# Attention and a two-layer product on one core: the first tiles of all batches first, wider late score runs, turned q left permuted

## The chip, the core and the metric

The kernel runs on one core of one Trainium2 chip. Its engines are TensorE (PE, matmuls), VectorE (DVE), ScalarE (ACT), GpSimd (POOL) and SyncE (SP); POOL, SP and ACT can also issue DMA transfers. The metric is the time of the program on the device in microseconds (us), as the median of several runs. The span of a profile goes from the first to the last instruction; the rest of the time lies around it.

## The reference

The inputs are q, k and v of 4 batches, 8 heads, 768 positions and 64 values a head. Attention is masked: a query sees the first 8 positions and the 96 positions up to its own, with a bias that falls with distance. The result goes through two matrix products with `h - tanh(h)` between them.

```python
scores = scale * np.matmul(q, k.transpose(0, 1, 3, 2))
dist = np.where(is_global & ~is_local, float(n_local), np.abs(rel))
scores = np.where(is_global | is_local, scores - slopes * dist, -1e9)
a = softmax(scores)
x = (a @ v).transpose(0, 2, 1, 3).reshape(3072, 512)
h = x @ w_in            # 512 x 2048
return (h - np.tanh(h)) @ w_out   # 2048 x 512
```

## The kernel before, in words

**Units.** The 3072 rows are 24 units of 128 positions, six a batch, taken in order: u = 0 to 23, with u % 6 the place i in the batch. A unit with i = 0 needs one block of keys (its own), every other unit two: its own (o = 0) and that of the unit before it (o = 1). The 8 global keys and values are copied from the batch's first unit over the first 8 places of the block (`a_K`, L436, `a_V`, L439, both through the copy helper at L302).

**Steps of a unit.** q and k are loaded by POOL's DMA queue with a cast to bf16 (`load_rows` L365 for units under `ROWS` = 4, which puts four consecutive positions in one partition's row; `load_natural` L368 for the others; unit 0 alone comes as f32 through SP and ACT and is cast by an engine). They are turned, so that the head's values lie along the partitions: units 0 to 5 by PE (`a_T`, L388, L392, L382) with a copy out of PSUM (`a_Te`, lines L300 on ACT and L302 on DVE), units 6 to 23 by a DMA transpose that SP issues (`a_DT`, L403). For units under `ROWS` the turned data come out in an order in which the four positions of a row are apart, and `a_Te` puts them in order while it copies. Then scores (`a_S`, L422; two heads at a time in the two halves of the partitions), exponential (`a_E`, L429), product with a mask that holds exp(bias) (`a_M`, L433; units under `BIASED` = 3 have the bias added on PE by `bias`, L346, instead), the product with v (`a_AV`, L448, with a column of ones that gives the sum), reciprocal and product (`a_R`, L456 and L457), and x turned again (`a_X`, L468, with a copy for units under 8; a DMA transpose, `a_DX`, L479, from unit 8 on). The three masks are made from PSUM at the start (`bm` through L346, `em` at L351).

**The two products.** Units form groups: 0 and 1 alone, then pairs. `m1` (L490) gives h for a group in pieces of 512 columns of one PSUM bank (128-column matmuls for a single unit, 256 for a pair), ACT takes tanh (L500), DVE subtracts (L506), `m2` (L515) sums 16 matmuls of 512 columns for a unit in one bank, ACT or DVE copies the bank out (L300, L302), and POOL or, for the last three units, SP stores it (L524). w_in comes in five pieces (in0 to in4: 2, 2, 4, 4 and 4 of the 16 row blocks), w_out in four (out0 to out3).

**The order.** It is made ahead by a planner (`Plan`, L17 to L191) that plays the operations through with a duration for each, a priority (`pri`, lower first), what they take and give back (the eight PSUM banks, in pairs for scores and AV; buffers; DMA lanes, eight for POOL's loads and stores, eight for SP's), and two rings for POOL's and SP's transfers that share the DMA engines equally. A transfer counts as landed after its issue, a lag, its work (`W_...`, L557), a tail and a slack (L21 and L22; it fades in from 20 to 30 us and out from 180 to 190 us). What the planner gives is the order of each engine's queue; on the chip each engine takes its queue strictly in that order and waits on semaphores. The list `first` (L576) sets POOL's loads by hand; then come kq and v of units 6 on. `AHEAD` (L558) lets the scores of unit u start only when `m1` has been issued up to unit u - 4.0, `T_AHEAD` (L562) lets its turn start from u - 6.0 on. `HOLD` keeps single operations back till a time, and dummy matmuls (L732) keep PE busy at the start. Numbers of buffers: `NK` 5 for loaded q and k, `NQK` 8 for turned ones, `NV` 10 for v, five for the exponentials, three for x.

Of the kernel before, what the change touches and what calls it, by code (L numbers as in the profile page):

```python
# [16 lines left out]
class Plan:  # L17
# [3 lines left out]
    SLACK_DMA = 2.5  # L21
    SLACK_DT = 6.0  # L22
# [33 lines left out]
    def run(self, free):  # L56
# [71 lines left out]
        while events:  # L128
            now, _, what, key = heapq.heappop(events)
            if what == "done":  # L130
                for g in ops[key]["give"]:
                    left[g] -= 1
                    if left[g] == 0:
                        h, part = g
                        p, ids = holds[h]
                        for i in ids if part is None else [ids[j] for j in part]:
                            avail[p].append((now, i))
                drop("done", key)
            elif what == "issued":
                drop("issue", key)  # L140
            elif what == "enter":
                flow(now)
                rings.setdefault(ops[key]["ring"], []).append([key, ops[key]["work"]])
                again(now)
            elif what == "flow":
                if key != version:
                    continue
                flow(now)
                for r in rings.values():
                    while r and r[0][1] <= 1e-9:  # L150
                        k, _ = r.pop(0)
                        push(now + ops[k]["tail"] + margin(now, self.SLACK_DT if k[0] in ("T", "Xe") else self.SLACK_DMA), "done", k)
                again(now)
            if events and events[0][0] <= now + 1e-9:
                continue
            for e in (PE, ACT, DVE, POOL, SP):
                if busy[e] > now + 1e-9:
                    continue
                best = None
                for k in ready[e]:  # L160
                    o = ops[k]
                    if best is not None and (o["pri"], o["n"]) >= best[0] or self.hold.get(k, 0.0) > now + 1e-9:
                        continue
                    if fits(o, now):
                        best = ((o["pri"], o["n"]), k)
                if best is None:
                    continue
                k = best[1]
                o = ops[k]
                for x in o["eng"]:  # L170
                    ready[x].remove(k)
                for h, p, n in o["take"]:
                    ids = self.choose(p, n, avail[p], now)
                    avail[p] = [g for g in avail[p] if g[1] not in ids]
                    holds[h] = (p, ids)
                us = o["us"] if e is o["eng"][0] or o["us2"] is None else o["us2"]
                if e is PE and now < self.cold:
                    us *= 2.0
                end = now + us
                busy[e] = end  # L180
                start[k] = now
                order.append((now, k, e))
                push(end, "free", e)
                push(end, "issued", k)
                if o["ring"] is None:
                    push(end + self.LAT[e] + margin(end, self.SLACK_ENG), "done", k)
                else:
                    push(end + o["lag"], "enter", k)
# [6 lines left out]
def kernel(  # L195
# [30 lines left out]
    PG = P // R4  # L226

    ROWS = 4
# [3 lines left out]
    BIASED = 3  # L232
    SINGLE = 2
    NK, NV, NQK = 5, 10, 8
# [109 lines left out]
    def bias(holder, o, m, stop):  # L344
        for a in range(2):
            nc.tensor.matmul(  # L346
                bank(holder, 2 * o + a), dist[:, m, :], slopes[:, a * NP : (a + 1) * NP, :], start=True, stop=stop
            )
# [10 lines left out]
    def rows_of(src, u):  # L359
        b, i = u // NQ, u % NQ  # L360
        return src[b, :, i * P : (i + 1) * P, :]
# [14 lines left out]
    def a_T(u):  # L376
        s = buf(("kq", u))
        for j in (1, 0):
            if u >= ROWS:
                t = bank(("tr", u, j)).bitcast(BF16)  # L380
                for p in range(NP):
                    nc.tensor.transpose(t[:, p * P : (p + 1) * P], s[:, j, p * P : (p + 1) * P], ident)  # L382
                continue
            t = bank(("tr", u, j))
            for r in range(R4):
                o = t[:, r * P : (r + 1) * P]
                if u < HW:
                    nc.tensor.matmul(o, s[:, j, r * P : (r + 1) * P], turn, start=True, stop=True)  # L388
                    continue
                for hh in range(2):  # L390
                    c = (hh * R4 + r) * Dh
                    nc.tensor.matmul(o[hh * Dh : (hh + 1) * Dh], s[:, j, c : c + Dh], turn, start=True, stop=True)  # L392

    def a_Te(e, u, j):
        t = bank(("tr", u, j))
        d = buf(("qk", u))[:, j]
        if u >= ROWS:
            copy(e, d, t.bitcast(BF16)[:, 0 : NP * P].rearrange("q (p f) -> q p f", p=NP))
        else:
            copy(e, d.rearrange("q p (g r) -> q r p g", r=R4), t.rearrange("q (r p g) -> q r p g", r=R4, p=NP))  # L400
# [6 lines left out]
    def blocks(u):  # L407
        return (0, 1) if u % NQ else (0,)

    def mask_of(u, o):  # L410
        return 2 if o else min(u % NQ, 1)

    def a_B(u):
        for o in blocks(u):
            bias(("s", u), o, mask_of(u, o), False)

    def a_S(u):
        for o in blocks(u):
            for p in range(NP):
                for hh in range(2):  # L420
                    r = slice(hh * Dh, (hh + 1) * Dh)
                    nc.tensor.matmul(  # L422
                        bank(("s", u), 2 * o + hh)[:, p * P : (p + 1) * P], buf(("qk", u - o))[r, 1, p, :],
                        buf(("qk", u))[r, 0, p, :], start=u >= BIASED, stop=u >= BIASED or p == NP - 1,
                    )

    def a_E(u, o):
        d = buf(("p", u, o)).rearrange("k (a h) f -> k a (h f)", a=2)
        nc.scalar.activation(d, banks(("s", u), 2 * o, 2 * o + 1), AF.Exp, bias=0.0, scale=scale)  # L429
# [5 lines left out]
    def a_K(e, u):  # L435
        copy(e, buf(("qk", u))[:, 1, :, 0:G], buf(("qk", u - u % NQ))[:, 1, :, 0:G])  # L436

    def a_V(e, u):
        copy(e, buf(("v", u))[0:G, :, 0:Dh], buf(("v", u - u % NQ))[0:G, :, 0:Dh])  # L439
# [4 lines left out]
    def a_AV(u):  # L444
        t = av(u)
        for h in range(H):
            for o in blocks(u):
                nc.tensor.matmul(  # L448
                    t[:, h // (H // 2), h % (H // 2), :], buf(("p", u, o))[:, slot(h), :], buf(("v", u - o))[:, h, :],
# [73 lines left out]
    def store(e, u, c0, c1):  # L523
        eng(e).dma_start(out=out[u * P : (u + 1) * P, c0:c1], in_=buf(("ot", u))[:, c0:c1])  # L524
# [9 lines left out]
    W_HW, W_ROW, W_NAT, W_WT, W_ST, W_DT, W_DX = 0.75, 0.69, 1.0, 2.54, 0.68, 1.2, 0.6  # L534
    AHEAD = 4.0
    BM_PRI = (45, -90, -89)
    EM_PRI = (45, 15, 25)
    HOLD = {('bm', 0): 20.0, ('M', 3, 0): 21.3}
    T_AHEAD = 6.0
# [11 lines left out]
    for m in range(3):  # L551
        op(("bm", m), PE, 0.44, lambda e, m=m: bias(("mk", m), 0, m, True),
# [23 lines left out]
    first = "v0 kq1 v1 kq2 v2 v3 in0 kq3 in1 in2 kq4 out0 v4 kq5 out1 in3 in4 v5 out2 out3"  # L576
# [36 lines left out]
    FLEX = (ACT, DVE)  # L613
    for u in range(NU):
        i = u % NQ
        b0 = u - i
# [5 lines left out]
        sdep = [("issue", go[-1])] if go else []  # L622
        kq_give = [(("kq", u), None)]
        if u < PE_T:
            op(("T", u), PE, 0.46, lambda e, u=u: a_T(u), after=tdep + [("turn" if u < ROWS else "ident",)],
               take=[(("tr", u, 0), "bank", 1), (("tr", u, 1), "bank", 1), (("qk", u), "qk", 1)], give=kq_give, pri=base)
            op(("Te", u, 1), (ACT, DVE), 0.6, lambda e, u=u: a_Te(e, u, 1), us2=0.72 if u < ROWS else 0.43, after=[("T", u)],
               give=[(("tr", u, 1), None)], pri=base)
            op(("Te", u, 0), (DVE, ACT), 0.7 if u < ROWS else 0.43, lambda e, u=u: a_Te(e, u, 0), us2=0.6,
               after=[("T", u)], give=[(("tr", u, 0), None)], pri=base)  # L630
            have = [("Te", u, 0), ("Te", u, 1)]
        else:
            op(("T", u), SP, 1.25, lambda e, u=u: a_DT(u), after=tdep,
               take=[(("qk", u), "qk", 1), (("lane", "T", u), "hlane", 1)], give=kq_give + [(("lane", "T", u), None)],
               pri=base, ring=SP, work=W_DT, lag=0.0, tail=D_TAIL)
            have = [("T", u)]
        nb = len(blocks(u))
        if u < BIASED:
            op(("B", u), PE, 0.43 * nb, lambda e, u=u: a_B(u), after=[("first",), ("slopes",), ("issue", ("S", u - 1)) if u else None, ("issue", ("T", u)) if u else None],
               take=[(("s", u), "bank", 2 * nb)], pri=base)  # L640
        last_user = i == NQ - 1
        s_give = [(("qk", u - 1), None)] if i >= 2 else []
        if last_user:
            s_give += [(("qk", u), None)]
        op(("S", u), PE, 0.23 * nb + 0.18, lambda e, u=u: a_S(u),
           after=have + sdep + [("K", u - 1) if i >= 2 else None, ("B", u) if u < BIASED else None],
           take=[] if u < BIASED else [(("s", u), "bank", 2 * nb)], give=s_give, pri=base)
        for o in blocks(u):
            op(("E", u, o), ACT, 1.03, lambda e, u=u, o=o: a_E(u, o), after=[("S", u)],
               take=[(("p", u, o), "pr", 1)], give=[(("s", u), (2 * o, 2 * o + 1))], pri=base)  # L650
# [3 lines left out]
        if 1 <= i < NQ - 1:  # L654
            op(("K", u), DVE, 0.16, lambda e, u=u: a_K(e, u), after=[("S", u)],
# [5 lines left out]
        if i >= 2:  # L661
            a_give += [(("v", u - 1), None)]
        if last_user:
            a_give += [(("v", u), None)]
        op(("AV", u), PE, 0.24 * nb, lambda e, u=u: a_AV(u),
           after=pm + [("lv", u), ("V", u - 1) if i >= 2 else None],
# [11 lines left out]
        else:  # L678
            op(("Xe", u), SP, 1.2, lambda e, u=u: a_DX(u), after=[("R", u)] + x_dep,
               take=x_take + [(("lane", "X", u), "hlane", 1)], give=[(("x", u), None), (("lane", "X", u), None)],  # L680
               pri=base, ring=SP, work=W_DX, lag=0.0, tail=D_TAIL)
# [106 lines left out]
```

## Time and profile before

| what | value |
|---|---|
| time, median of 3 runs | 215.45 us (215.19 to 215.81) |
| time of the profiled execution | 215.66 us |
| its span | 213.7 us |
| PE, DVE, ACT, POOL busy | 204.3, 128.0, 120.0, 79.9 us |
| first row of L490 / of L515 on PE | 16.69 / 25.14 us |
| last PE matmul ends | 210.86 us |
| transposes on SP: of q and k / of x | 18 / 16 |
| matmuls of L346 (bias) recorded | 14 of 16 |

The page of the profile lists the busy time of each engine, 40 equal slices of the span with a digit for the busy tenths, the chain of work that ended last, and the costliest groups of instructions: source line, engine, operation, tiles, count, busy time and mean duration, then the idle time of the engine just before them with what ended it. L12 is line 12 of the kernel. A matmul's own duration holds the time through the array, so durations of neighbours overlap; what one costs in a stream is read from the chain, where pieces follow each other without overlap. A few matmul records are missing from the trace. PEld is the load of weights into the array, which runs beside the matmuls.

### The profile page before, as it was taken

The page shows a single profiled execution, that of the slowest core. Times are in us where ns is not written, and L with a number is a line of the kernel's source. Part 1 is how long each engine was busy: PE and PEld are TensorE (multiplying, and loading weights), DVE is VectorE, ACT ScalarE, POOL GpSimd, SP SyncE. Part 2 cuts the span into 40 slices and gives each one's busy share as a digit, 9 for nine tenths or more (in the row PEclk, how much of TensorE's full clock was granted, in tenths as well). Part 3 has the DMA queues.
Part 4 walks back from the last instruction along what each step waited for, and adds up shares of the span by engine and source line. Part 5 has one row for each costly group of instructions (what it writes and reads, how often), then busy time and mean ns, then how long its engine had stood idle before and what let it go on. Part 6 is the DMA issues. An engine that isn't in the chain of part 4 may idle for free.

```text
span 213.7 us, 5020 instructions
## 1 busy us (share of the span) xinstructions
PE 204.3 (96%) x2043; PEld 141.3 (66%) x2062; DVE 128.0 (60%) x256; ACT 120.0 (56%) x177; POOL 79.9 (37%) x105
## 2 busy tenths in 40 slices
PE   7679899999999999999999999999999999999994
PEld 2448686858656966856856865856856866848643
DVE  6588974834666985974881880853881880813600
ACT  4869855556576674753923923753923923715421
POOL 8996364467476454624537252001002002011000
PEclk9999999999999999999999999999999999999999
DMA  5999999999999999999999999915513012102012
GB/s 115 157 182 188 183 207 198 168 145 155 186 148 196 139 174 127 160 138 143 179 113 207 120 186 191 205 29 130 94 25 93 35 25 81 44 0 98 3 49 98
DMA packets 103478, 27.32 MB, mean 128 GB/s; under 512 B 94944, under 2 KB 101856, under 8 KB 103456
## 3 DMA queue, kind: packets, MB, share of 16 engines
q0 software_dynamic: 74624, 18.88, 90.6%
q1 hardware_dynamic: 28560, 7.87, 28.9%
q8 instruction: 16, 0.26, 0.5%
q10 hardware_dynamic: 272, 0.26, 0.5%
q14 instruction: 6, 0.05, 0.1%
HBM read 27.26 MB, written 6.29 MB: 157 GB/s over the span
## 4 chain that ended last, share of the span: by engine, by line
PE 86%; POOL 6%; DMA 5%; issue 1%; ACT 0%; POOLq 0%
PE ps L515 39%; PE ps L490 38%; DMA w_out_bf<-in_moe_w_out_dram 5%; PE ps L422 5%; PE ps L448 4%; POOL kq L365 2%; POOL vb L368 2%; POOL w_in_bf L371 1%; POOL kq L368 1%; PE ps L468 0%; PE ps L382 0%; POOL rel L306 0%; ACT ot L300 0%; POOLq L306 0%; POOLq L769 0%
## 5 line engine op out<-in xcount | busy, mean ns | idle before, releaser
L490 PE MATMUL ps<-xT,w_in_bf 128*128 128x256 bf16 (+1 forms) x832 | 89.5, 264 | 0.1
L515 PE MATMUL ps<-w_out_bf,g 128*128 128x512 bf16 (+2 forms) x383 | 86.1, 370 | 1.3 <-DMA w_out_bf<-in_moe_w_out_dram 0.3
L490 PEld LDWEIGHTS <-w_in_bf 128*128 128x128 bf16 x832 | 75.1, 98 | 12.0
L506 DVE TENSOR_TENSOR g<-ps,th 128x512 bf16<-128x512 f32 x96 | 64.0, 685 | 31.2 <-ACT th L500 30.1
L500 ACT ACTIVATE th<-ps 128x512 f32<-128x512 f32 x96 | 55.9, 605 | 23.8 <-PE ps L490 23.1
L515 PEld LDWEIGHTS <-g 128*128 128x128 bf16 x400 | 36.9, 98 | 38.8 <-issue 0.4
L429 ACT ACTIVATE pr<-ps 128x1024 bf16<-128x1024 f32 x44 | 42.9, 1023 | 8.1 <-PE ps L422 8.0
L300 ACT COPY ot<-ps 128x512 f32<-128x512 f32 (+2 forms) x22 | 12.5, 567 | 54.2 <-PE ps L515 54.2
L524 POOL DMA_DIRECT2D out_dram<-ot x21 | 11.8, 561 | 68.6 <-ACT ot L300 61.9
L433 DVE TENSOR_TENSOR pr<-pr,mk 128x1024 bf16<-128x1024 bf16 x39 | 26.4, 687 | 8.9 <-ACT pr L429 8.8
L368 POOL DMA_DIRECT2D vb<-in_v_dram x24 | 21.7, 905 | 12.1 <-DMA kq<-in_q_dram 2.6
L368 POOL DMA_DIRECT2D kq<-in_k_dram x20 | 17.7, 885 | 16.8 <-DMA kq<-in_k_dram 8.5
L368 POOL DMA_DIRECT2D kq<-in_q_dram x20 | 17.6, 882 | 11.7 <-DMA kq<-in_k_dram 5.3
L457 DVE TENSOR_TENSOR x<-ps,rden 128x512 bf16<-128x512 f32 x24 | 16.6, 692 | 0.8
L448 PEld LDWEIGHTS <-pr 128*128 128x128 bf16 x352 | 13.6, 97 | 3.7 <-ACT pr L429 1.1
L448 PE MATMUL ps<-vb,pr 128*128 128x65 bf16 x352 | 14.6, 193 | 0.8 <-DVE qk L302 0.8
L422 PEld LDWEIGHTS <-qk 64*128 64x128 bf16 x352 | 10.2, 94 | 7.2 <-issue 5.4
L456 DVE RECIPROCAL rden<-ps 128x8 f32<-128x8 f32 x24 | 5.0, 207 | 12.2 <-PE ps L448 11.5
L302 DVE COPY qk<-qk 128x32 bf16<-128x32 bf16 x16 | 2.8, 176 | 15.5 <-PE ps L422 15.3
L422 PE MATMUL ps<-qk 64*128 64x128 bf16 x192 | 9.5, 218 | 2.3 <-ACT qk L300 1.8
L302 DVE CAST qk<-ps 128x512 bf16<-128x512 f32 x5 | 6.3, 1305 | 2.9 <-PE ps L388 1.6
L422 PE MATMUL ps<-qk,qk 64*128 64x128 bf16 x160 | 7.8, 216 | 0.0
(43 smaller groups left out, 59.0 us busy)
## 6 DMA issues: line engine op xcount, KB each, us to landing
out_dram<-ot POOLq DMA_DIRECT2D x21, 256.0 KB, 7.2
vb<-in_v_dram POOLq DMA_DIRECT2D x24, 128.0 KB, 11.2
kq<-in_k_dram POOLq DMA_DIRECT2D x23, 128.0 KB, 11.3
kq<-in_q_dram POOLq DMA_DIRECT2D x23, 128.0 KB, 10.5
w_out_bf<-in_moe_w_out_dram POOLq DMA_DIRECT2D x4, 512.0 KB, 12.3
w_in_bf<-in_moe_w_in_dram POOLq DMA_DIRECT2D x3, 512.0 KB, 12.1
w_in_bf<-in_moe_w_in_dram POOLq DMA_DIRECT2D x2, 256.0 KB, 6.4
out_dram<-ot SPq DMA_DIRECT2D x2, 256.0 KB, 2.0
```

What stands on the lines that cost most here:

```text
L300: nc.scalar.copy(out=out, in_=in_)
L368: eng(e).dma_start(out=dst, in_=rows_of(src, u).rearrange("h p d -> p h d"))
L422: nc.tensor.matmul(bank(("s", u), 2 * o + hh)[:, p * P : (p + 1) * P], buf(("qk", u - o))[r, 1, p, :], buf(("qk", u))[r, 0, p, :], start=u ...
L429: nc.scalar.activation(d, banks(("s", u), 2 * o, 2 * o + 1), AF.Exp, bias=0.0, scale=scale)
L433: nc.vector.tensor_tensor(out=t, in0=t, in1=mk[:, mask_of(u, o)], op=ALU.mult)
L448: nc.tensor.matmul(t[:, h // (H // 2), h % (H // 2), :], buf(("p", u, o))[:, slot(h), :], buf(("v", u - o))[:, h, :], start=o == 0, stop=o ...
L457: nc.vector.tensor_tensor(out=buf(("x", u)).rearrange("q (a h) d -> q a h d", a=2), in0=t[:, :, :, 0:Dh], in1=rden.to_broadcast([P, 2, H / ...
L490: nc.tensor.matmul(t[:, (f - f0) * n : (f - f0 + 1) * n], w_in_bf[j][:, c, fo : fo + P], x[:, c, 0:n], start=(c == 0), stop=(c == CD - 1),)
L500: nc.scalar.activation(h_view(buf(("th", g, f0)), g, m), h_view(bank(("h", g, f0)), g, m), AF.Tanh, bias=0.0, scale=1.0)
L506: nc.vector.tensor_tensor(out=buf(("g", g))[:, f0 : f0 + m, 0:n], in0=h_view(bank(("h", g, f0)), g, m), in1=h_view(buf(("th", g, f0)), g, ...
L515: nc.tensor.matmul(bank(part)[:, 0 : c1 - c0], buf(("g", g))[:, f, t * P : (t + 1) * P], w_out_bf[f // FJ][:, f % FJ, c0:c1], start=(f == ...
L524: eng(e).dma_start(out=out[u * P : (u + 1) * P, c0:c1], in_=buf(("ot", u))[:, c0:c1])
```

## The change

Six things are changed.

1. The units are taken in another order: `turn_of` lists the first tiles of the four batches first (u = 0 to 3), then the other five of each batch. `nth` is the place in the batch, `back` the unit before in the batch, `head` the batch's first unit. So the first four units have one block each, and the first tiles' k and v are kept until their batch is through (`NQK` 11, `NV` 12). `BIASED` is 4; the mask for first tiles is not made, since no unit from 4 on uses it.
2. From unit 16 on, scores run in threes of blocks: of three units, two runs instead of three. Scores of a block have banks of their own (`("s", u, o)`).
3. `ROWS` is 5. For these units k is turned straight into its order (PE writes PSUM with a step of four), q stays in the turned order, `a_Te` copies both without rearranging, and `a_S` reads q through `queries`, which jumps 128 elements between neighbouring columns.
4. POOL's loads come in another order at the start.
5. The planner's figures are new: slacks 1.5 and 3.0 instead of 2.5 and 6.0, with 2.5 more for a transpose when another ring is at work; transposes have 0.8 of lag and works of 1.66 and 1.18 instead of 1.2 and 0.6; a store 0.6 instead of 0.68; a turn on PE 0.69 instead of 0.46; `AHEAD` 4.5, `T_AHEAD` 5.5; other priorities for the masks, other `HOLD`s.
6. The planner may keep an operation that needs many banks ahead of lower ones (`KEEP` = 9); no operation takes more than six.

```diff
-    SLACK_DMA = 2.5
-    SLACK_DT = 6.0
+    SLACK_DMA = 1.5
+    SLACK_DT = 3.0
+    SHARED = 2.5
+    KEEP = 9
...
-                        push(now + ops[k]["tail"] + margin(now, self.SLACK_DT if k[0] in ("T", "Xe") else self.SLACK_DMA), "done", k)
+                        more = margin(now, self.SLACK_DMA)
+                        if k[0] in ("T", "Xe"):
+                            shared = any(x for y, x in rings.items() if y is not e)
+                            more = margin(now, self.SLACK_DT) + (self.SHARED if shared else 0.0)
+                        push(now + ops[k]["tail"] + more, "done", k)
...
-    ROWS = 4
+    ROWS = 5
-    BIASED = 3
+    BIASED = 4
-    NK, NV, NQK = 5, 10, 8
+    NK, NV, NQK = 5, 12, 11
+    turn_of = sorted(range(NU), key=lambda t: (t % NQ > 0, t))
+    nth = [t % NQ for t in turn_of]
+    back = [turn_of.index(t - 1) if t % NQ else None for t in turn_of]
+    head = [turn_of.index(t - t % NQ) for t in turn_of]
+    THREES = 16
...
+        if u < THREES or u + 2 >= NU:
+            runs.append([(u, o) for o in blocks_of(u)])
+            u += 1
+        else:
+            runs += [[(u, 0), (u, 1), (u + 1, 0)], [(u + 1, 1), (u + 2, 0), (u + 2, 1)]]
+            u += 3
...
-                o = t[:, r * P : (r + 1) * P]
+                o = t.rearrange("q (p g r) -> q r p g", r=R4, p=NP)[:, r] if j else t[:, r * P : (r + 1) * P]
...
-            copy(e, d.rearrange("q p (g r) -> q r p g", r=R4), t.rearrange("q (r p g) -> q r p g", r=R4, p=NP))
+        copy(e, d, t if u < ROWS else t.bitcast(BF16)[:, 0 : NP * P])
+
+    def queries(u, p, r):
+        d = buf(("qk", u))[r, 0]
+        if u < ROWS:
+            return d.rearrange("q p f -> q (p f)").rearrange("q (r p g) -> q p g r", r=R4, p=NP)[:, p]
+        return d[:, p]
...
-                        buf(("qk", u))[r, 0, p, :], start=u >= BIASED, stop=u >= BIASED or p == NP - 1,
+                        queries(u, p, r), start=u >= BIASED, stop=u >= BIASED or p == NP - 1,
...
-    W_HW, W_ROW, W_NAT, W_WT, W_ST, W_DT, W_DX = 0.75, 0.69, 1.0, 2.54, 0.68, 1.2, 0.6
-    AHEAD = 4.0
-    BM_PRI = (45, -90, -89)
-    EM_PRI = (45, 15, 25)
-    HOLD = {('bm', 0): 20.0, ('M', 3, 0): 21.3}
-    T_AHEAD = 6.0
+    W_HW, W_ROW, W_NAT, W_WT, W_ST, W_DT, W_DX = 0.75, 0.69, 1.0, 2.54, 0.6, 1.66, 1.18
+    AHEAD = 4.5
+    BM_PRI = (-88,-90,-89)
+    EM_PRI = (45,2,35)
+    HOLD = {('m2', 1, 0, 2): 43.5, ('g', 2, 6): 31.8, ('Te', 1, 0): 8.0, ('Te', 1, 1): 8.0}
+    T_AHEAD = 5.5
...
-    for m in range(3):
+    for m in range(3) if BIASED < 4 else (1, 2):
...
-    first = "v0 kq1 v1 kq2 v2 v3 in0 kq3 in1 in2 kq4 out0 v4 kq5 out1 in3 in4 v5 out2 out3"
+    first = "kq1 v0 v1 kq2 kq3 v2 v3 kq4 in0 in1 out0 in2 in3 v4 out1 kq5 in4 v5 out2 out3"
...
+                op(("S", n), PE, 0.23 * len(xs) + 0.18, lambda e, xs=xs: a_S(xs), after=s_after[n] + s_dep[first_u],
+                   take=s_take[n], give=s_give[n], pri=10.0 * first_u)
...
-               pri=base, ring=SP, work=W_DT, lag=0.0, tail=D_TAIL)
+               pri=base, ring=SP, work=W_DT, lag=0.8, tail=D_TAIL)
-               pri=base, ring=SP, work=W_DX, lag=0.0, tail=D_TAIL)
+               pri=base, ring=SP, work=W_DX, lag=0.8, tail=D_TAIL)
```

## The prediction

> **What bounds the kernel now.** I read the busy times and the 40 slices first, then the table of stretches, then TensorE's rows in order of time, then the DMA issues.
>
> ```profile
> PE 204.3 (96%) x2043; PEld 141.3 (66%) x2062; DVE 128.0 (60%) x256; ACT 120.0 (56%) x177; POOL 79.9 (37%) x105
> ...
> PE   7679899999999999999999999999999999999994
> ```
>
> TensorE (PE) is busy 96% of the span; the rest lies in the first five slices and in the last. The table of stretches (its first columns are the stretch, its length, and PE's busy time) says the same in microseconds:
>
> ```profile
> 5.00:16.70 11.70, 8.34 (x140) 5.52 (x139) 7.59 (x13) 9.12 (x11) 11.17 (x16) 1.00 1.59 169
> 16.70:25.10 8.40, 7.52 (x148) 6.86 (x147) 7.35 (x17) 7.94 (x12) 4.00 (x6) 1.00 1.80 181
> 25.10:45.00 19.90, 19.70 (x220) 15.09 (x223) 13.24 (x25) 11.03 (x18) 11.13 (x13) 1.00 1.67 188
> 45.00:140.00 95.00, 94.33 (x947) 65.83 (x956) 62.50 (x118) 56.43 (x85) 45.13 (x57) 1.00 1.82 162
> 140.00:210.90 70.90, 70.58 (x587) 46.84 (x589) 33.98 (x60) 33.13 (x54) 4.32 (x8) 1.00 0.20 55
> ```
>
> From 25.1 to 210.9 PE lacks 0.2 + 0.7 + 0.3 = 1.2 us in 185.8. So the end is fixed by when PE becomes full and by how much work is then left. Nothing can be won after 25.1 except by removing PE work; much can be lost there. TensorE's rows of the first stretch (start, time, what, in brackets the idle time before and who ended it):
>
> ```profile
> 7.86 0.40 PE L422 MATMUL ps<-qk 64*128 64x128 bf16 x8 [1.48 <-ACT qk L300]
> ...
> 14.12 0.64 PE L448 MATMUL ps<-vb,pr 128*128 128x65 bf16 x16 [0.78 <-DVE qk L302]
> ...
> 16.69 1.09 PE L490 MATMUL ps<-xT,w_in_bf 128*128 128x128 bf16 x16
> ...
> 20.90 0.38 PE L346 MATMUL ps<-slopes,dist 128*128 128x512 bf16 x1
> ...
> 25.14 1.89 PE L515 MATMUL ps<-w_out_bf,g 128*128 128x512 bf16 x7 [0.33 <-DMA w_out_bf<-in_moe_w_out_dram]
> ```
>
> Two things are seen. Up to 16.7 PE waits for turned q and k. From 16.7 to 25.1 it has the first matrix product of units 0 and 1 only; the second starts when the first piece of w_out lands. For prices I take pieces of the chain that ended last, where PE runs without a gap:
>
> ```profile
> 41.11 0.48 PE ps L448 x16
> ...
> 45.29 3.45 PE ps L515 x16
> 48.74 6.99 PE ps L490 x64
> ...
> 132.34 0.33 PE ps L422 x8
> ...
> 139.15 0.55 PE ps L422 x16
> ```
>
> A 512-column matmul takes 0.216 us, a 256-column one 0.109, a 128-column one of L490 half of that (0.055). A score run of one block costs 0.33, of two 0.55, so 0.11 fixed and 0.22 a block. AV (L448) costs 0.48 for two blocks, and 0.26 for one (the chain has 0.26 for x8). A transposition of x costs 0.22 (x4).
>
> **The stretch 16.7 to 25.1 of before.** Counted work: 64 small matmuls of L490, 3.50; two score runs, 1.10; two AV, 0.96; two x, 0.44; the transposes of unit 4, 0.45; the two bias matmuls for mask 0, 0.43. Sum 6.88 of 8.40, so 1.52 are lost to waits and unfilled starts.
>
> **First tiles first.** Units 0 to 3 are now the first tiles of the four batches, with one block each: four blocks stand before group 2 is complete, where before it was seven. Bias matmuls fall from 16 (10 for units 0 to 2, 6 for masks) to 12 (8 and 4). The mask-0 pair at 20.9 goes, which is 0.43 in a stretch that is nearly full; the other two go from waiting time and count nothing. ScalarE loses one mask exponential (1.02), VectorE gains one mask product (0.69); neither is near its limit (56% and 60%).
>
> **When the data come.** Each load, asked singly for issue and landing: v0 is issued at 1.36 and lands at 7.0, then k1 7.9, q1 8.5, v1 9.6, k2 10.2, q2 10.8, v2 11.8, v3 12.7, in0 14.4, k3 15.1, q3 15.8, in1 17.1, in2 19.6, k4 20.4, q4 21.3, out0 25.1. Up to v3 the lag is 5.0 to 5.6, so POOL's issues (0.70 for rows, 0.88 natural, 0.45 more for the first) set the pace; later the transfer does: 0.7 a row load, 1.3 for 256 KB, 2.5 for 512 KB (out0: 3.8). In the new order I get k1 6.6, q1 7.6, v0 8.7, v1 9.5, k2 10.0, q2 10.7, k3 11.4, q3 12.2, v2 13.1, v3 14.0, k4 14.7, q4 15.4, in0 16.9, in1 18.2, out0 20.7 to 22.0, in2 23.2 to 24.5. So w_out comes 3 to 4 us earlier, w_in 1.1 later, and 2.5 more us of loads for units 3 and 4 stand ahead of it.
>
> PE can be full from about 17.8 (before, L490 started 0.4 ahead of in1 as well). Is unit 3 ready? q3 12.2, turn 0.64, latency 0.2, copy 0.69, scores 0.33, exponential 1.03 and 0.2, AV 0.26 and 0.2, reciprocal and product 0.90, x 0.42, copy 0.6: about 17.7; groups 0 and 1 have 1.75 us of L490 before it, so there is some slack. Done by 17.8 and not by 16.7 in before: unit 4's turn (0.45), scores 4 x 0.33 + 0.55 = 1.87 against 1.43, AV 1.04 against 0.74, two more x (0.44): 1.63 us of work for 1.1 us of time, +0.53.
>
> From 17.8 the supply is: L490 on in0 and in1 for four units, 16 x 4 x 4 x 0.055 = 3.5, with AV and x of unit 4 (0.7), to 22.0; out0 is there, 16 x 0.216 = 3.45, to 25.4; in2 is there, 3.5. In3 (about 26), out1 (29), in4 (34), out2 (37), out3 (40) each bring another 3.5, so arrival stays ahead. Of the 1.52 lost I let 0.6 come back: the joint at 22 is tight, and four open w_out sums hold four of eight PSUM banks. Bounds are 0 and 1.52.
>
> **Turned q stays permuted.** The casts go from a strided write to a contiguous one:
>
> ```profile
> L302 DVE CAST qk<-ps 128x512 bf16<-128x512 f32 x5 | 6.3, 1305 | 2.9 <-PE ps L388 1.6 <-PE ps L392 1.3
> L300 ACT CAST qk<-ps 128x512 bf16<-128x512 f32 x3 | 3.9, 1299 | 0.0
> ...
> L302 DVE COPY ot<-ps 128x512 f32<-128x512 f32 x3 | 2.1, 692 | 0.5 <-PE ps L515 0.5
> ```
>
> So about 0.6 off each of eight casts; unit 4's two go from 0.42 and 0.59 to about 0.65 each. This shortens the chain of a unit, but data arrive too late for it to move 17.8, so I count nothing. If loads came sooner it would be worth 0.6. The price moves to PE: k is written into PSUM with steps of four elements (36 half or whole matmuls), and q is read with a jump of 128 elements at each column (48 score matmuls). No row of before has a strided PE operand. The nearest rows are the casts above, where a step of four costs a factor 1.9; the other end is no cost, and a gain is excluded, because the same columns pass. At 1.9, scores 48 x 0.034 x 0.9 = 1.5 and turns 36 x 0.04 x 0.9 = 1.3. Nearly all of it falls before 17.8, where PE has some 3.4 us idle, so I take 0, and keep up to 1.5 for the range.
>
> The Trainium skill, page "Advanced Engine Details and Errata", section "Memory Cachelines", speaks against this part: SBUF is fast only where accesses share a 16-byte line, and any PSUM pattern that is not contiguous slows matmuls significantly. It gives no figure, and the casts' 1.9 is the only size that this trace offers for a stride; the rule is rival 1 below.
>
> **Late runs of three.** From unit 16 on, two sets of three units need two runs of three blocks instead of three of two: 2 x (0.77) against 3 x 0.55, 0.11 a set, 0.22 in all, on the path. Such a run wants three free bank pairs of four. Its exponentials free them at 1.03 steps, so one bank is left to L490 for about 1.25 us, which is at most 0.4 lost a run, 1.6 for four runs; at these places w_out work, which needs one bank, can stand beside, so I take 0.
>
> **Transposes planned anew.** This changes only the order: a score run may follow its transpose by one unit of MLP progress instead of two (4.5 against 5.5, before 4.0 against 6.0; a unit is some 7.9 us). The planned time to landing becomes 1.25 + 0.8 + 1.66 + 0.95 + 3.0 = 7.7 alone, and 11.8 when loads share the engines. Measured from issue to landing:
>
> ```profile
> qk<-kq SPq DMA_TRANSPOSE x16, 10.1
> xT<-x SPq DMA_TRANSPOSE x11, 8.4
> ```
>
> This is the answer for 40 to 138 us, with 11.5 as the longest; after 138 it is 3.8 and 2.4. The planned 11.8 covers it, so I count 0 while loads run.
>
> **Sum.** 1.52 - 0.6 + 0.43 + 0.53 + 0.22 = 2.1 us. The profiled execution took 215.66 with a span of 213.7; the span should become 211.6. The median, 215.45, is 0.2 below that execution; I take the gain off the median: **213.4**.
>
> **Rivals.** (1) Strides cost PE time that is not hidden: the factor 1.9 lengthens unit 3's chain by 0.3 for the turn, 0.3 for scores, and unit 4's turn and scores by 0.8, which fall near 17.8. Gain 2.1 - 1.1 = 1.0: 214.4. For it: the casts; against it: idle PE until 17.8. This is what the rule cited above makes of the time. (2) Weights come late: w_in 19.0 and out0 with its 3.8 again, so that the whole 1.52 is lost again, only elsewhere; 2.1 - 0.9 - 0.8 = 0.4: 215.0. For it: POOL is busy 11.17 of 11.7 us from 5 to 16.7, so any delay there moves all loads. (3) Slower: the score run stands in PE's order before its transpose has landed. In before it starts 13 to 18 us after the issue; one unit less is 5 to 10, and only the plan's wait holds it back. Where the plan takes the engines to be free and they are not, PE stalls 10.1 - 7.7 = 2.4, and behind it wait all of PE's matmuls. One such wait eats the gain; two give 215.45 - 2.1 + 4.8 = 218.1. Against it: loads fill the DMA engines until 138 us on the chip, and in a plan with nearly the same work too. (4) That the change does less than said: the start is bound by loads alone, and PE's lost time stays; this ends as (2).
>
> **Numbers.** Forecast 0.60 (212.2 to 214.7); rival 1 0.12; rivals 2 and 4 0.13; rival 3 0.15. A measurement of this kernel tells 0.3%, 0.65 us, from no change. Faster: 0.60 + 0.12 = 0.72; within: 0.13; slower: 0.15. The range goes from 212.2 (nothing comes back of the 1.52, and unit 4's AV done early) to 215.9, which leaves out rival 3 and little more.
>
> **What would show it.** Right: PE's first row of L490 near 17.8, of L515 before 22.5, full from there; casts near 0.65; L422 rows of three blocks taking 0.77; no PE idle time over 0.3 us after 25. Wrong: L422 rows of units 0 to 4 with more than 0.045 us a matmul (rival 1); idle PE ended by w_in or w_out after 18 (rival 2); idle PE ended by a transpose's qk or xT between 45 and 138 (rival 3).

## The result, and the profile after

The changed kernel takes 216.56 us (median of 22 runs), the kernel before in the same runs 215.83: ratio 1.0037, 95% interval 1.0024 to 1.005. It is slower by 0.7 us where 2.1 faster was forecast, and lies above the stated range (212.2 to 215.9). The first profiled execution (span 213.6, time 215.74) is the lowest of the 22, so by itself it hides the loss; a second one lies higher and is shown in experiment 5.

The table of stretches, whose rows answer to those of before (PE's busy time is the number behind the stretch's length, the granted clock the third from the right):

```profile
5.00:16.70 11.70, 10.89 (x129) 6.11 (x128) 4.91 (x9) 7.81 (x12) 11.70 (x17) 1.00 1.54 150
16.70:25.10 8.40, 8.15 (x103) 6.23 (x102) 6.27 (x13) 6.11 (x9) 3.88 (x5) 1.00 1.26 201
25.10:45.00 19.90, 19.80 (x239) 15.33 (x239) 13.09 (x24) 10.06 (x16) 10.01 (x13) 1.00 1.78 183
45.00:140.00 95.00, 94.31 (x977) 66.56 (x986) 63.47 (x121) 58.28 (x85) 45.74 (x57) 1.00 1.93 161
140.00:210.90 70.90, 70.38 (x599) 47.24 (x603) 37.25 (x67) 33.00 (x51) 4.35 (x8) 1.00 0.19 57
```

PE is now busy 10.89 of 11.7 us before 16.7, against 8.34, and 8.15 of 8.4 in the next stretch, against 7.52; from 25.1 on it is as full as before. The time did not go into waits. PE's rows in order of time show what it was busy with (L449 is the score line, L517 the first product, L542 the second; other kernels have other line numbers):

```profile
7.31 1.03 PE L449 MATMUL ps<-qk 64*128 64x128 bf16 x8
...
8.81 1.04 PE L449 MATMUL ps<-qk 64*128 64x128 bf16 x8
...
18.47 1.04 PE L449 MATMUL ps<-qk 64*128 64x128 bf16 x8 [0.20 <-DVE qk L326]
19.32 1.06 PE L449 MATMUL ps<-qk,qk 64*128 64x128 bf16 x8
20.31 1.07 PE L517 MATMUL ps<-xT,w_in_bf 128*128 128x128 bf16 x16
...
24.08 1.89 PE L542 MATMUL ps<-w_out_bf,g 128*128 128x512 bf16 x7
```

The same in pieces of the chain that ended last, which from 3.1 on is mostly PE: a run of one block for unit 0, of two for unit 4, of two for unit 5 (whose q is not permuted), and of three.

```profile
7.38 0.96 PE ps L449 x8
...
18.47 1.91 PE ps L449 x16
...
37.64 0.55 PE ps L449 x16
...
124.81 0.78 PE ps L449 x24
```

Sixteen score matmuls take 1.91 us where q is read with jumps and 0.55 where it is not. Over the 48 of units 0 to 4, the steps from one matmul to the next, without waits, add up to 5.71 us, against 2.01 in the first experiment below: 0.119 each against 0.042. Each run has some 0.1 more at its end in both; in the longer runs of the later stream a step is 0.034. The first product starts at 20.31, not at 17.8, although its second piece of w_in had landed at 19.1.

The casts are what they were to be: 0.69 us on VectorE and 0.59 on ScalarE, where the kernel before has 1.31 and 1.30. So part 3 moved a cost from two engines with room to the one without.

### The profile page after: what moved, and what is told of

Same layout as the page of the kernel before. It is cut to its first block, busy times and chain, and to the rows that moved or that the text cites. A ratio compares the mean times of both kernels' runs of the same rounds, so it can differ in the third digit from the quotient of the medians.

```text
span 213.6 us, 5023 instructions
## 1 busy us (share of the span) xinstructions
PE 207.3 (97%) x2045; PEld 142.6 (67%) x2066; DVE 128.3 (60%) x262; ACT 117.6 (55%) x173; POOL 79.5 (37%) x105
## 4 chain that ended last, share of the span: by engine, by line
PE 95%; DVE 2%; issue 1%; ACT 1%; POOL 0%; POOLq 0%; DVEq 0%
PE ps L517 40%; PE ps L542 39%; PE ps L449 8%; PE ps L475 5%; PE ps L370 2%; PE ps L416 1%; PE ps L495 1%; ACT pr L456 0%; DVE slopes L360 0%; PE ps L412 0%; DVE x L484 0%; DVE qk L326 0%; PE ps L407 0%; DVE far L336 0%; PE ps L766 0%
## 5 line engine op out<-in xcount | busy, mean ns | idle before, releaser
L517 PE MATMUL ps<-xT,w_in_bf 128*128 128x256 bf16 (+1 forms) x832 | 88.7, 264 | 0.1
L542 PE MATMUL ps<-w_out_bf,g 128*128 128x512 bf16 (+2 forms) x380 | 85.8, 370 | 1.2 <-issue 0.3
L517 PEld LDWEIGHTS <-w_in_bf 128*128 128x128 bf16 x832 | 74.7, 98 | 10.2 <-issue 0.4
L527 ACT ACTIVATE th<-ps 128x512 f32<-128x512 f32 x96 | 56.6, 602 | 30.2 <-PE ps L517 28.1
L542 PEld LDWEIGHTS <-g 128*128 128x128 bf16 x400 | 37.3, 98 | 38.7
L456 ACT ACTIVATE pr<-ps 128x1024 bf16<-128x1024 f32 x44 | 42.7, 1024 | 19.2 <-PE ps L449 17.8
L324 ACT COPY ot<-ps 128x512 f32<-128x512 f32 (+2 forms) x19 | 10.7, 563 | 38.1 <-PE ps L542 37.5
L392 POOL DMA_DIRECT2D kq<-in_k_dram x19 | 16.9, 887 | 11.9 <-DMA kq<-in_k_dram 5.2
L392 POOL DMA_DIRECT2D kq<-in_q_dram x19 | 16.9, 888 | 11.7 <-DMA kq<-in_k_dram 4.0
L475 PEld LDWEIGHTS <-pr 128*128 128x128 bf16 x352 | 13.5, 97 | 4.5 <-ACT pr L456 1.7
L449 PEld LDWEIGHTS <-qk 64*128 64x128 bf16 x352 | 10.8, 96 | 7.8 <-issue 5.9
L475 PE MATMUL ps<-vb,pr 128*128 128x65 bf16 x352 | 14.7, 193 | 0.8 <-ACT pr L456 0.8
L449 PE MATMUL ps<-qk 64*128 64x128 bf16 x192 | 12.7, 254 | 0.2 <-DVE qk L326 0.2
L449 PE MATMUL ps<-qk,qk 64*128 64x128 bf16 x160 | 8.4, 225 | 0.0
L326 DVE COPY ot<-ps 128x512 f32<-128x512 f32 x6 | 4.1, 692 | 4.2 <-PE ps L542 4.2
```

Source lines behind the costliest of these rows:

```text
L324: nc.scalar.copy(out=out, in_=in_)
L392: eng(e).dma_start(out=dst, in_=rows_of(src, u).rearrange("h p d -> p h d"))
L449: nc.tensor.matmul(bank(("s", u, o), hh)[:, p * P : (p + 1) * P], buf(("qk", back[u] if o else u))[r, 1, p, :], queries(u, p, r), start=u ...
L456: nc.scalar.activation(d, banks(("s", u, o), 0, 1), AF.Exp, bias=0.0, scale=scale)
L475: nc.tensor.matmul(t[:, h // (H // 2), h % (H // 2), :], buf(("p", u, o))[:, slot(h), :], buf(("v", back[u] if o else u))[:, h, :], start= ...
L517: nc.tensor.matmul(t[:, (f - f0) * n : (f - f0 + 1) * n], w_in_bf[j][:, c, fo : fo + P], x[:, c, 0:n], start=(c == 0), stop=(c == CD - 1),)
```

## The experiments

Theory A: TensorE's jumping reads of q ate the gain. Rivals: the loads set the start whatever PE does; the order of the middle costs something in some executions; single parts of the change bring nothing. Every ratio is to the kernel before, run beside it on the same chip (its median was 215.65 to 215.85).

**1. q turned in PSUM too.** The changed kernel; `a_T` puts q in order as it does k, `queries` returns the contiguous slice.

```diff
-                o = t.rearrange("q (p g r) -> q r p g", r=R4, p=NP)[:, r] if j else t[:, r * P : (r + 1) * P]
+                o = t.rearrange("q (p g r) -> q r p g", r=R4, p=NP)[:, r]
...
-        if u < ROWS:
-            return d.rearrange("q p f -> q (p f)").rearrange("q (r p g) -> q p g r", r=R4, p=NP)[:, p]
```

> The changed kernel, with q of units 0 to 4 turned into natural order in PSUM as k is (the turn writes with a step of four), so that the scores read q contiguously; the order of all instructions stays. Theory A (the strided reading of q by TensorE ate the gain): score matmuls of units 0 to 4 go from 0.121 back to about 0.035 us, 3.9 us less of TensorE in the first 20 us; the turns grow by at most 0.14 each; the first row of the first product goes from 20.3 to about 18.7, set by the second piece of w_in (landed at 19.1), and the time falls by about 1.5, to 215.0. Rival (the loads set the start, whatever TensorE does): first product at 20 and the time stays within 0.4 of the changed kernel. Rival (a strided write into PSUM is as dear as the strided read): turns grow by 0.6 each and the time stays.

Measured: 214.28 us, ratio 0.993 (0.9908 to 0.9953); 2.0 below the changed kernel beside it (216.28). Its PE rows (L447 scores, L416 a turn, L515 the first product):

```profile
7.73 0.40 PE L447 MATMUL ps<-qk 64*128 64x128 bf16 x8
...
15.38 1.17 PE L416 MATMUL ps<-turn,kq 128*64 128x128 bf16 x16
...
17.34 0.40 PE L447 MATMUL ps<-qk 64*128 64x128 bf16 x8 [0.20 <-DVE qk L326]
17.56 0.40 PE L447 MATMUL ps<-qk,qk 64*128 64x128 bf16 x8
17.89 1.28 PE L515 MATMUL ps<-xT,w_in_bf 128*128 128x128 bf16 x16
```

The first product starts at 17.89, where the prediction had 17.8; the 18.7 expected here was too late, since PE begins on the first piece of w_in (landed at 17.0) before the second (18.5). Theory A holds: the scores take 3.7 us less, the turns 1.1 more (steps of a 64-column turn 0.064 against 0.050), and of the 2.6 that remain 2.4 arrive at the first product and 2.0 in the time. PE's waits from 9 to 18 us are 1.13, in the changed kernel 0.95 up to 20.3: so idle time had taken up 0.2 of the dearer scores. The order of all instructions is that of the changed kernel.

**2. Part 3 alone, on the kernel before** (units 0 to 3, order untouched).

```diff
-                o = t[:, r * P : (r + 1) * P]
+                o = t.rearrange("q (p g r) -> q r p g", r=R4, p=NP)[:, r] if j else t[:, r * P : (r + 1) * P]
...
+        copy(e, d, t if u < ROWS else t.bitcast(BF16)[:, 0 : NP * P])
...
-                        buf(("qk", u))[r, 0, p, :], start=u >= BIASED, stop=u >= BIASED or p == NP - 1,
+                        queries(u, p, r), start=u >= BIASED, stop=u >= BIASED or p == NP - 1,
```

> The kernel before with part 3 of the change alone: for units 0 to 3 k is turned into order in PSUM, q stays permuted, the copies are contiguous, scores read q with jumps; everything else, the order too, as before. Theory A: 56 score matmuls go from 0.036 to 0.121, 4.8 us more of TensorE before 20 us, against some 3.4 us of idle time there and copies that are 0.6 shorter: slower by 1 to 3, about 217.5. Rival (strides cost nothing that shows, as the prediction counted): within 0.4 of the kernel before, or faster by up to 0.6.

Measured: 218.66, ratio 1.0129 (1.0107 to 1.015), 2.8 slower. The casts fell to 0.69 and 0.58, and the scores of the first 25 us (L425) did this:

```profile
L425 PE MATMUL ps<-qk 64*128 64x128 bf16 x32 | 4.1, 389 | 0.7 <-ACT qk L300 0.7
L425 PE MATMUL ps<-qk,qk 64*128 64x128 bf16 x24 | 3.2, 393 | 0.0
```

7.3 us of PE in 56 matmuls. Part 3 alone is worse than the whole change (216.28 in the same series), so with it in place the other parts together gain.

**3. The permutation in the copy's reading side.** The turns write PSUM contiguously, the copies read PSUM with jumps and write SBUF contiguously, the scores read contiguously.

```diff
-                o = t.rearrange("q (p g r) -> q r p g", r=R4, p=NP)[:, r] if j else t[:, r * P : (r + 1) * P]
+                o = t[:, r * P : (r + 1) * P]
...
+            copy(e, d.rearrange("q p (g r) -> q p g r", r=R4), t.rearrange("q (r p g) -> q p g r", r=R4, p=NP))
...
-        if u < ROWS:
-            return d.rearrange("q p f -> q (p f)").rearrange("q (r p g) -> q p g r", r=R4, p=NP)[:, p]
```

> The changed kernel with the permutation put into the copies' reading side: for units 0 to 4 the turns write PSUM contiguously, the copy reads PSUM with jumps and writes SBUF contiguously, the scores read contiguously; order unchanged. Here neither TensorE operand is strided. If the copies' 1.30 us in the kernel before came from the strided writing into SBUF, they stay near 0.60 and 0.69, the turns of 16 fall from 0.98 to about 0.64, and the time falls from 214.3 (q turned in PSUM) to about 213.6. If reading PSUM with jumps is as dear for ScalarE and VectorE, the copies take 1.3 and the time is 214.3 to 215.0.

Measured: 214.78, ratio 0.9952 (0.9936 to 0.9968). The casts:

```profile
L326 DVE CAST qk<-ps 128x512 bf16<-128x512 f32 x5 | 3.4, 690 | 4.0 <-PE ps L412 2.6 <-PE ps L416 1.1
L324 ACT CAST qk<-ps 128x512 bf16<-128x512 f32 x5 | 2.8, 587 | 2.2 <-PE ps L416 1.3 <-PE ps L412 0.8
```

They take 0.69 and 0.59, as contiguous ones do: reading PSUM with jumps costs these engines nothing that shows; the 1.30 of before was the strided writing into SBUF. The turns fall to 0.040 a step. PE has about 1.5 us less work than in experiment 1, yet the time is not lower. In the profiled execution the clock fell:

```profile
14.00:17.40 3.40, 1.89 (x42) 1.34 (x42) 1.15 (x3) 1.98 (x3) 2.79 (x5) 1.00 1.33 180
17.40:20.80 3.40, 3.35 (x41) 2.98 (x39) 2.32 (x5) 2.54 (x4) 2.32 (x3) 0.50 1.20 185
```

After 3.4 us in which PE was busy only 1.89, the clock stood at half for the next 3.4. This is not the reason, though: three of the six executions show the drop in their mean clock (0.992), with a median of 214.81, and the three without it have 214.75.

**4. The same with dummies in the gap.**

```diff
+            if u == 4 and not j:
+                for _ in range(5):
+                    nc.tensor.matmul(t, zero[:, 0, :], zero.to_broadcast([P, 4, P]), start=True, stop=True)
```

> The kernel whose copies read PSUM permuted, with five dummy matmuls of 512 columns on zeros ahead of unit 4's turn of q, where TensorE waited 1.23 us for the load and the granted clock then stood at half from 17.4 to 20.8 in its profiled execution. If low activity of TensorE before 17.4 cost the clock, no execution shows a mean clock of 0.992 (three of six did) and the time falls from 214.8 to about 214.0. If the dummies do not count, or the loads set the pace anyway, the time stays at 214.8 or rises by up to 1.1, the dummies' own length.

Measured: 214.57, ratio 0.9948 (0.9931 to 0.9966); none of 12 executions has a mean clock under 1.0. The clock part is as expected; the time is only 0.2 lower, inside the spread, where 0.8 was expected. The profile shows a wait for a load (L521 is the first product):

```profile
24.66 4.62 PE L521 MATMUL ps<-xT,w_in_bf 128*128 128x128 bf16 x72 [0.95 <-DMA w_in_bf<-in_moe_w_in_dram]
```

PE, now early, waits 0.95 us for the third piece of w_in, which landed at 24.62. In experiment 1 the piece landed at 23.58 and PE's work on it began at 23.62. So there too PE came only 0.04 behind the landing: as long as the piece lands then, cheaper turns can bring nothing before it. Why it landed 1.0 later here is open. Experiments 1, 7 and this one are the best versions; their intervals overlap.

**5. The changed kernel once more**, no edit.

> The changed kernel once more, unaltered, for a second profiled execution beside the kernels below. In its first profiled execution the span was 213.6 us, the lowest of 22, while the median time was 216.56. If something in the middle of the kernel differs from execution to execution (a score run that comes before its transpose has landed: rival 3 of the prediction), an execution near the median shows TensorE idle by 0.5 us or more somewhere after 25 us, ended by a transpose's tile. If only the start differs, the idle time or the extra time lies before 25 us.

Measured: 216.28, ratio 1.0036 (1.0015 to 1.0057). The profiled execution took 217.24. After 25 us PE is as full as in the first profile; the difference is ahead of it:

```profile
7.60:11.00 3.40, 2.64 (x27) 0.94 (x24) 1.16 (x3) 2.23 (x3) 3.40 (x5) 1.00 1.43 157
11.00:14.40 3.40, 3.18 (x31) 2.59 (x33) 1.85 (x4) 1.17 (x2) 3.40 (x6) 0.50 1.88 170
14.40:17.80 3.40, 3.40 (x38) 1.62 (x36) 1.12 (x2) 1.61 (x2) 3.04 (x4) 1.00 1.35 184
```

The stretch 7.6 to 11 holds two jumping score runs and a wait of 0.76; the next has half the clock, and the first product starts at 21.85. So the start differs, not the middle. The first profiled execution has the same stretch, and no drop behind it:

```profile
7.60:11.00 3.40, 2.64 (x27) 0.94 (x24) 1.16 (x3) 2.23 (x3) 3.40 (x5) 1.00 1.44 166
11.00:14.40 3.40, 3.35 (x55) 2.63 (x58) 2.53 (x6) 1.72 (x3) 3.40 (x6) 1.00 1.74 152
```

So the work in the stretch does not decide alone; what differs between the two executions is not shown. Over both series, 9 of 34 executions have the lower mean clock (0.992) and a median of 217.25, the other 25 a median of 216.3; the kernel before shows none in 29 executions. The drop explains part of the loss; without it about 0.5 us remain.

**6. The changed kernel with four such dummies ahead of unit 1's AV.**

```diff
         t = av(u)
+        if u == 1:
+            for _ in range(4):
+                nc.tensor.matmul(bank(("av", u)), zero[:, 0, :], zero.to_broadcast([P, 4, P]), start=True, stop=True)
```

> The changed kernel with four dummy matmuls of 512 columns on zeros ahead of unit 1's AV, in the 0.76 us in which TensorE waits for an exponential. In the second profiled execution of the changed kernel the granted clock was at half from 11.02 to 14.43, and 9 of 34 executions show a mean of 0.992 and about 217.25 against 216.3. If low activity of TensorE just before 11 us is the cause, no execution shows 0.992 and the median is 216.1 or lower; if the wait is not what decides, about a quarter still do and the median is 216.3 to 216.6.

Measured: 216.16, ratio 1.0023 (1.0009 to 1.0038); none of 12 executions has the lower clock, where 9 of 34 had. The time is 0.06 above the most that was expected. With experiment 4 (none of 12, where 3 of 6 had it) this shows that work for PE in the wait keeps the clock up. It does not show a threshold: in experiment 11 PE is busy 1.66 us from 49.53 to 52.94, in the kernel before 1.93 from 4.93 to 8.34, and no drop follows.

**7. No runs of three** (on experiment 1).

```diff
-    THREES = 16
+    THREES = NU
```

> q turned in PSUM, and no score runs of three blocks: every unit has its own run. The prediction's term: two runs less of fixed 0.11 each, so 0.2 slower than with them, 214.5. If the runs of three squeeze the PSUM banks (0.4 each, four of them), it is faster instead, by up to 1.4.

Measured: 214.28, ratio 0.9937 (0.9923 to 0.9952). No difference from experiment 1. Each run of three took 0.78 in the changed kernel, as counted, but neither the 0.2 nor a bank squeeze can be told from zero.

**8. The units in the old order** (on 7).

```diff
-    BIASED = 4
+    BIASED = 3
...
-    turn_of = sorted(range(NU), key=lambda t: (t % NQ > 0, t))
+    turn_of = list(range(NU))
```

> As the one without runs of three, and with the units in the order of before (the first tile of a batch just before its other tiles; bias on TensorE for units 0 to 2, three masks); POOL's loads keep the new order. The prediction's terms for the unit order (0.43 of bias, and the work that can stand before the first product, 0.53, with some of the lost 1.52): 1.0 to 1.8 slower than the one without runs of three, near 215.8. If the new unit order brings nothing, the two are within 0.3.

Measured: 218.16, ratio 1.0107 (1.0087 to 1.0127), 3.9 slower than 7. More than expected: PE is busy 6.68 of 8.40 us from 16.7 to 25.1, with 1.18 of idle time ended by w_in, and 0.67 at 54.06 that belongs to the order planned for it. The load list was not made for this unit order, so the 3.9 are not the unit order's alone.

**9. The loads in the old order** (on 1).

```diff
-    first = "kq1 v0 v1 kq2 kq3 v2 v3 kq4 in0 in1 out0 in2 in3 v4 out1 kq5 in4 v5 out2 out3"
+    first = "v0 kq1 v1 kq2 v2 v3 in0 kq3 in1 in2 kq4 out0 v4 kq5 out1 in3 in4 v5 out2 out3"
```

> q turned in PSUM, with the load order of before, the rest of the change as it is. Rival 2 of the prediction says that the weights behind two more units' loads cost the start: then this is within 0.3 or faster, since the second piece of w_in lands at 17 instead of 18.5 and w_out at 25 instead of 21. If early w_out is what lets TensorE fill up, this loses what the kernel before lost between 17 and 25 (up to 1.5), 215.0 to 215.8.

Measured: 215.71, ratio 1.0005 (0.9994 to 1.0017), 1.4 slower than 1. The second piece of w_in landed at 17.3 (18.5 in experiment 1), the first of w_out at 23.7 (21.0). PE's first row of the second product is this:

```profile
25.48 1.04 PE L540 MATMUL ps<-w_out_bf,g 128*128 128x512 bf16 x3
```

It stands 1.8 us behind the landing, so not the load alone but also the order planned for this list holds it back. The new list as a whole is worth 1.4; how much of it is early w_out, and what late w_in costs, is not separated. Rival 2 of the prediction, that the new list costs the start more than it brings, falls.

**10. The old planning figures on the changed kernel** (the lags of the transposes too).

```diff
-    SLACK_DMA = 1.5
-    SLACK_DT = 3.0
-    SHARED = 2.5
+    SLACK_DMA = 2.5
+    SLACK_DT = 6.0
+    SHARED = 0.0
...
-    W_HW, W_ROW, W_NAT, W_WT, W_ST, W_DT, W_DX = 0.75, 0.69, 1.0, 2.54, 0.6, 1.66, 1.18
-    AHEAD = 4.5
+    W_HW, W_ROW, W_NAT, W_WT, W_ST, W_DT, W_DX = 0.75, 0.69, 1.0, 2.54, 0.68, 1.2, 0.6
+    AHEAD = 4.0
...
-    T_AHEAD = 5.5
+    T_AHEAD = 6.0
```

> The changed kernel planned with the slacks, the lags and works of transposes and stores and the two AHEAD values of before; the order differs. Theory A: the same strided reads, the same start, the time within 0.5 of the changed kernel's. Rival 3 (the new figures let score runs stand before their transposes in some executions): the median falls by 0.5 or more and the times of single executions lie closer together.

Measured: 218.93, ratio 1.0144 (1.0109 to 1.0178), 2.6 slower than the changed kernel. Both expectations fail: the order has a hole (L475 is AV, L495 the turn of x).

```profile
51.68 0.63 PE L475 MATMUL ps<-vb,pr 128*128 128x65 bf16 x15 [0.23 <-DVE pr L460]
53.33 0.40 PE L495 MATMUL ps<-ident,x 128*128 128x128 bf16 x4 [1.03 <-DVE x L484]
54.40 3.39 PE L517 MATMUL ps<-xT,w_in_bf 128*128 128x256 bf16 x16 [0.68 <-ACT xT L324]
```

AV of a unit, its x and the product that needs it stand directly behind each other, and PE waits 1.9 us with nothing between; the clock at half from 54.6 to 58.0 follows in this execution. Three of the six have the lower mean clock (219.55 to 220.34); the other three take 218.11 to 218.30, some 1.8 more than the changed kernel without the drop (216.3).

**11. Two pieces of w_in ahead of unit 4's loads** (on 4).

```diff
-    first = "kq1 v0 v1 kq2 kq3 v2 v3 kq4 in0 in1 out0 in2 in3 v4 out1 kq5 in4 v5 out2 out3"
+    first = "kq1 v0 v1 kq2 kq3 v2 v3 in0 in1 kq4 out0 in2 in3 v4 out1 kq5 in4 v5 out2 out3"
```

> The kernel with copies that read permuted and with the dummies, and with the two first pieces of w_in loaded before unit 4's k and q instead of behind them; planned anew with that list. The second piece of w_in lands at about 17.4 instead of 18.5 to 19.4, and the first product can start 1 us earlier. If loads of weights set the start (what is left of rival 2): 0.5 to 1.0 faster than without, near 213.3. If the attention of unit 4 is then missing as work, or the order falls out worse, the same or slower by up to 1.

Measured: 217.24, ratio 1.0077 (1.0059 to 1.0095), 2.7 slower than 4. The order made with that list has the same hole (1.03 and 0.67 at 51.5 and 52.5), and PE waits 0.72 for w_in at 17.6. Its first product starts at 16.25, but whether the loads alone would gain in time is left open.

**12. The kernel before with copies that read permuted**, nothing else.

```diff
-            copy(e, d.rearrange("q p (g r) -> q r p g", r=R4), t.rearrange("q (r p g) -> q r p g", r=R4, p=NP))
+            copy(e, d.rearrange("q p (g r) -> q p g r", r=R4), t.rearrange("q (r p g) -> q p g r", r=R4, p=NP))
```

> The kernel before with one edit: the copies of units 0 to 3 read PSUM with jumps and write SBUF contiguously; order and all else as before. The eight casts fall from 1.30 to 0.60 and 0.69. By the prediction (data arrive too late for a shorter chain to matter before the first product, at most 0.6 to win) 215.2 to 215.8. If the casts were what TensorE waited for before 16.7 (it idles 3.4 us there), up to 1.5 faster, 214.3.

Measured: 215.05, ratio 0.9979 (0.9957 to 1.0): 0.75 faster in the medians, at the edge of the interval and a little below the 215.2 to 215.8 expected; the 214.3 of the other expectation is far off. One of the 12 executions has the lower clock (217.07).

```profile
7.80 0.40 PE L422 MATMUL ps<-qk 64*128 64x128 bf16 x8 [0.67 <-ACT qk L300]
```

PE's wait before its first scores falls from 1.48 to 0.67, and PE then waits 0.52 for w_in at 17.1.

## Why the prediction was wrong, point by point

- **What bounds the kernel**: right. PE is full from 25 us on in both, and the start decides.
- **The step that failed**: "Nearly all of it falls before 17.8, where PE has some 3.4 us idle, so I take 0." The 3.4 us were those of the kernel before. In the new order with contiguous q (experiment 1) PE is busy 11.61 of the 12.8 us from 5.0 to 17.8, and its waits hardly shrink when the scores get dearer: of 2.6 us more work 2.4 went into the start of the first product, which came at 20.3. The price was too small as well. I had 1.5 us for the scores as the dear end, from the casts' factor 1.9; the trace gives 3.7 (0.119 against 0.042). The turns of k were priced too high: 1.3 as the dear end, about 0.6 measured (against experiment 4). Rival 1 named the mechanism, and its 214.4 carried the factor 1.9; its three terms (0.3, 0.3 and 0.8) add up to 1.4, while 1.1 was taken off without a reason. With 20.3 in place of 17.8, the 2.1 become -0.4, against about -0.5 measured where the clock holds.
- **The rule weighed there.** The Trainium skill, "Advanced Engine Details and Errata", section "Memory Cachelines", says that SBUF is fast only where accesses share a 16-byte line and that any PSUM pattern that is not contiguous slows matmuls significantly. The traces agree with both halves. Here the 256-byte jumps in the moving operand (the one that streams through the array) cost a factor 2.8 beside the same place's contiguous reads, 3.5 in runs of two blocks (1.91 against 0.55); a PSUM write in steps of 16 bytes cost a turn 0.064 against 0.043 or less. So SBUF's half was the dearer. No run varies the length of the jump. Treating a rule without a figure as a rival at one nearest factor was not enough.
- **The clock**: not in the prediction. Part of the executions lose about 0.9 us to one stretch at half clock. The Trainium skill, "TensorE: Matmul & The Clock Gate", part 1, puts the drop to an idle window of about 3.4 us; here no idle time was longer than 0.76 (experiment 5), and PE was busy 2.64 of 3.4. So such an idle time is not needed for a drop, by the measurement; what is, stays open.
- **When the data come**: right within 0.9 us (second piece of w_in 18.2 predicted, 19.1 in the changed kernel and 18.5 in experiment 1; w_out 20.7 to 22.0, measured 21.7 and 21.0). PE full near 17.8: right in experiment 1.
- **w_out early**: the sign is right for the new list as a whole, 1.4 against the 0.9 counted (1.52 - 0.6); the share of w_out was not isolated (experiment 9).
- **Shorter casts**: counted as nothing, at most 0.6; 0.75 on the kernel before, with an interval that reaches no change (experiment 12).
- **Bias and unit order**: the sign is right, the size was not isolated (experiment 8).
- **Runs of three**: 0.22 counted, none seen.
- **Transposes planned anew**: right that nothing waits for them. After 25 us no wait of PE over 0.2 us, and the transposes' time to landing stayed (10.3 and 8.0 from 40 to 138 us, before 10.1 and 8.4). One reading was short: in the kernel before the score runs start 13 to 23 us after the issue, not 13 to 18. The figures do matter through the order: with the old ones a hole of 1.9 us opens, which I had not counted as a gain of this part.
- With the scores' jumps gone, experiment 1 gains 1.6 (215.85 beside it, to 214.28), of 2.1. The rest is open. The forecast time itself was too low by 0.4 more, since its base was 215.45, the median of three runs, where 22 give 215.83.

## What to carry to other kernels

A permutation costs on whichever operand takes the jump, so try each place: here TensorE's moving read was dearest, a strided SBUF write by ScalarE or VectorE doubled the copy, TensorE's PSUM write cost half as much again, and the copies' PSUM read was free. Idle time of the bound engine in the old kernel does not cover an extra cost in the new one; work out the new order as a chain, wait by wait, not as a sum. When an order is made by a planner, look for holes in the order before crediting a size to a part.

## What the runs showed of the hardware

- Score matmuls of 128 columns, two at a time in the two halves of the partitions, step 0.119 us on average when neighbouring columns of the moving operand lie 256 bytes apart (changed kernel), 0.042 in the same place without jumps (experiment 1).
- A 64-column turn steps 0.040 to 0.043 us when it writes PSUM contiguously (experiments 3 and 4), 0.064 when it writes in steps of 16 bytes (experiment 1).
- A 128 x 512 cast from PSUM takes 0.59 (ScalarE) and 0.69 (VectorE), contiguous (changed kernel) or reading PSUM with jumps (experiment 3), and 1.30 when it writes SBUF in steps of 8 bytes (kernel before).
- The granted clock fell to 0.50 for 3.4 us after stretches in which TensorE was busy 2.64 or 1.89 of 3.4 us, with no idle time over 1.23 (experiments 5 and 3). The same 2.64 was followed by no drop in another execution of the same kernel, nor were 1.93 (kernel before) and 1.66 (experiment 11). A few dummy matmuls in the wait left no drop in 24 executions, where 9 of 34 and 3 of 6 had one.
